# Two MLPs behind hashed attention on one core: products with v in threes, a narrower hash with bits through DRAM, 128-row rounding, copies per PSUM tile

## The chip, the cores and the metric

The kernel runs on one core of a Trainium2 chip. The metric is the device time of one execution in microseconds, as the median of repeated runs.

## What is computed

Attention for 2 batches of 8 heads (16 heads of 768 positions, width 64). Six random projections of q and of k give each position a 6-bit bucket; a score counts only where the buckets of the two positions agree. Then two MLPs over 1536 tokens (512 to 2048 to 512), the first with softplus, the second with hard swish.

```python
q_bits = (np.einsum('bhsd,dk->bhsk', q, proj) > 0)      # 6 bits; likewise k_bits
mask = q_bucket[:, :, :, None] == k_bucket[:, :, None, :]
scores = scale * np.matmul(q, k.transpose(0, 1, 3, 2))
scores = np.where(mask, scores, -1000000000.0)
attn = softmax(scores);  x = attn @ v                    # to (1536, 512)
h = x @ w1_in;  x = softplus(h) @ w1_out
h = x @ w2_in;  out = (h * np.clip(h + 3, 0, 6) / 6) @ w2_out
```

## The kernel before

A planner (`Schedule.run`) writes out the instruction order of every engine before anything runs: each operation has a cost per engine, a due time (`prio`, from `WHEN`, `TH`, `STEP`, ...) and dependencies, and the planner repeatedly gives the engine that would end first its most urgent operation that is ready. `SAME` and `CROSS` are what it charges from an operation's end to its follower on the same or on another engine, `STAY` what a change between kinds of matmul (scores, transposes, column tiles) adds to the due time. Each engine then runs its list strictly in order.

*Preparation of a head* (`prepare`, lines 302 to 415). Numbers are split into a rounded high part and a remainder, so that matmuls of the fast type keep precision. `raw` holds k in rows 0 to 63 and q in rows 64 to 127, `rawk` holds k twice. ACT writes q's high part scaled (line 337) and k's high part twice (`ka`, line 249). DVE writes q's remainder (line 344) and k's remainder (line 254, `kb`) in two 64-row operations. One DMA copies q's high part to `qb` (line 366). The hash (line 379) multiplies `raw` with a sign matrix into two 64-column tiles of 384 columns, side by side in PSUM; DVE turns the sums into bits (line 401, `bt`), and four DMAs spread the bits over rows 64 to 95 of `qb` and `kb` (line 410). Head 0 has no time for DMAs: its four quarters of bits are written by DVE (line 391), each from 32 rows.

*Attention of a head* (`attend`, lines 420 to 536), in six tiles of 128 queries. Two matmuls per half of the keys give the scores (lines 437 and 438; the second one has remainders and bits, and takes the mask into the sum). DVE takes the maximum (451) and makes scale and bias for the exponential (458), ACT the exponential (466), TensorE six transposes (477), ACT or, for every third tile, ACT or DVE the copy into `et` (line 249 or 251). Products with v (493) run in column tiles of 64, two side by side, in groups of two key chunks, eight records each. Then the result goes through a copy, a transpose back (515) and the division (530), and every second head into the features `xh`, `xl` (557 and on).

*PSUM* has three double banks (`two0` to `two2`), which scores and transposes take in turn, so that three tiles form a batch, and two single banks (`av`, `pre`) for the products with v, the hash and the other transposes.

*The MLPs* run over 2 layers, 3 groups of 512 tokens and 16 slices of the hidden width: 12 matmuls into `ph` (662), the activation on ACT and DVE, 12 accumulating matmuls into two double banks (755 in the first layer, 757 in the second). Weights arrive as 64-bit floats and are converted on ACT and DVE; half of the first layer's blocks are converted during attention, the rest behind it. At a group's end `finish` copies the four sums of 512 columns one by one.

## Time and profile before

| what | value |
|---|---|
| median of 3 runs | 785.51 us (785.46 to 785.63) |
| profiled execution: its own time | 787.35 us |
| its span, first instruction to last | 785.6 us |
| granted TensorE clock, mean | 0.998 |
| PE busy | 764.9 us, 97% |
| DVE busy | 529.0 us, 67% |
| ACT busy | 485.0 us, 62% |

The span is what the engines' instructions cover; the profiled execution takes 1.7 us more around it. Busy shares are means over stages that differ: attention up to some 245 us, the MLPs behind it. A matmul's end is modelled, so TensorE counts as busy through short waits; the start of the next instruction tells more than the length of one.

### The profile page before, as it was taken

How to read it: one execution, taken by the hardware profiler on the slowest of the kernel's cores; microseconds unless marked ns; L12 is line 12 of the kernel's file. 1: busy time of each engine (PE TensorE's matmuls, PEld its weight loads, DVE VectorE, ACT ScalarE, POOL GpSimd, SP SyncE). 2: the span in 40 equal slices, each digit the busy share in tenths (PEclk: the TensorE clock that was granted, in tenths of full speed). 3: DMA queues.
4: the chain of work that ended last, by engine and by line, in shares of the span. 5: the costliest groups of instructions: out<-in, count | busy, mean ns of one | idle time of the engine just before them, and what ended most of it. 6: DMA issues, size and time to landing. Idle time of an engine off the chain costs nothing.

```text
span 785.6 us, 10356 instructions
## 1 busy us (share of the span) xinstructions
PE 764.9 (97%) x3808; PEld 599.1 (76%) x3808; DVE 529.0 (67%) x938; ACT 485.0 (62%) x821; POOL 9.5 (1%) x53
## 2 busy tenths in 40 slices
PE   4999999999999999999999999999999999999997
PEld 2677677677668788878888788878888888888886
DVE  6698887888986999964545899999932222232222
ACT  3789999998988778665556678766622322232222
POOL 1000000000000000000000000000000000000000
PEclk9999999999999999999999999999999999999999
DMA  5354454353323070000000555530000100010001
GB/s 165 108 162 116 115 165 120 110 163 118 80 73 134 28 294 1 1 0 1 1 0 1 188 196 191 177 107 1 1 0 14 42 0 1 1 53 1 1 0 54
DMA packets 26354, 58.61 MB, mean 75 GB/s; under 512 B 3584, under 2 KB 7552, under 8 KB 26304
## 3 DMA queue, kind: packets, MB, share of 16 engines
q1 hardware_dynamic: 22128, 49.56, 19.7%
q10 hardware_dynamic: 4176, 8.39, 3.4%
q8 instruction: 30, 0.49, 0.3%
q14 instruction: 20, 0.16, 0.1%
HBM read 48.89 MB, written 3.15 MB: 66 GB/s over the span
## 4 chain that ended last, share of the span: by engine, by line
PE 90%; ACT 4%; DVE 3%; issue 2%; DMA 1%; SPq 0%; ACTq 0%; DVEq 0%
PE ph L662 34%; PE acc L755 17%; PE acc L757 17%; PE tp L477 7%; PE av L493 6%; PE sc L437 4%; PE sc L438 3%; ACT e L466 2%; DVE nm L451 2%; PE xt L557 1%; ACT ka L249 1%; PE pt L515 1%; PE d L379 1%; DMA raw<-in_q_dram 1%; ACT et L249 0%
## 5 line engine op out<-in xcount | busy, mean ns | idle before, releaser
L662 PE MATMUL ph<-xh,w 128*128 128x512 f32 x768 | 239.1, 393 | 0.0
L662 PEld LDWEIGHTS ph<-xh,w 128*128 128x128 f32 x768 | 143.8, 188 | 31.7
L662 PE MATMUL ph<-xl,w 128*128 128x512 f32 x384 | 150.2, 391 | 0.0
L691 DVE SCALAR_TENSOR_TENSOR ml<-me,ph 128x512 f32<-128x512 f32 x48 | 33.1, 690 | 116.0 <-ACT me L686 115.8
L686 ACT ACTIVATE me<-ph,three 128x512 f32<-128x512 f32 x48 | 33.0, 687 | 124.2 <-PE ph L662 120.7
L466 ACT ACTIVATE e<-sc,bs 128x768 f32<-128x768 f32 x96 | 94.0, 986 | 19.0 <-DVE bs L458 19.0
L451 DVE TENSOR_REDUCE nm<-sc 128x1 f32<-128x768 f32 x96 | 88.7, 951 | 20.8 <-PE sc L438 20.6
L755 PE MATMUL acc<-gh,w 128*128 128x512 f32 x384 | 98.8, 395 | 0.1
L757 PE MATMUL acc<-w,gh 128*128 128x512 f32 x384 | 97.4, 392 | 0.0
L477 PEld LDWEIGHTS tp<-ident,e 128*128 128x128 f32 x576 | 63.3, 142 | 29.3 <-ACT e L466 20.2
L755 PEld LDWEIGHTS acc<-gh,w 128*128 128x128 f32 x384 | 70.9, 188 | 19.1 <-ACT gh L249 2.8
L757 PEld LDWEIGHTS acc<-w,gh 128*128 128x128 f32 x384 | 72.1, 188 | 16.2
L662 PEld LDWEIGHTS ph<-xl,w 128*128 128x128 f32 x384 | 72.1, 188 | 16.0
L477 PE MATMUL tp<-ident,e 128*128 128x128 f32 x576 | 76.6, 281 | 4.9 <-ACT e L466 3.8
L437 PE MATMUL sc<-ka,qa 128*128 128x384 f32 x192 | 69.1, 360 | 0.1
L493 PE MATMUL av<-et,vx 128*64 128x384 f32 x384 | 68.8, 494 | 0.0
L438 PE MATMUL sc<-kb,qb 96*128 96x384 f32 x192 | 65.3, 340 | 0.8 <-DVE kb L391 0.7
L249 ACT ACTIVATE et<-tp 128x768 f32<-128x768 f32 x82 | 62.2, 815 | 2.4 <-PE tp L477 2.3
L722 DVE SCALAR_TENSOR_TENSOR me<-mu,me 128x512 f32<-128x512 f32 x48 | 33.3, 693 | 33.1 <-ACT mu L717 33.0
L249 ACT ACTIVATE gh<-ml 128x512 fp32r<-128x512 f32 x48 | 30.2, 629 | 38.8 <-DVE ml L734 38.6
L755 PE MATMUL acc<-gl,w 128*128 128x512 f32 x192 | 53.4, 392 | 0.7 <-ACT xh L249 0.7
L757 PE MATMUL acc<-w,gl 128*128 128x512 f32 x192 | 53.1, 391 | 0.0
(65 smaller groups left out, 957.8 us busy)
## 6 DMA issues: line engine op xcount, KB each, us to landing
raw<-in_moe_w_out_dram SPq DMA_DIRECT2D x30, 512.0 KB, 3.5
raw<-in_moe_w_in_dram SPq DMA_DIRECT2D x18, 512.0 KB, 4.3
raw<-in_moe_w_in_dram ACTq DMA_DIRECT2D x14, 512.0 KB, 4.8
rawk<-in_kv_dram SPq DMA_DIRECT2D x15, 384.0 KB, 5.0
raw<-in_kv_dram SPq DMA_DIRECT2D x16, 192.0 KB, 3.2
raw<-in_q_dram SPq DMA_DIRECT2D x16, 192.0 KB, 3.7
vx<-in_kv_dram SPq DMA_DIRECT2D x16, 192.0 KB, 3.0
out_dram<-y SPq DMA_DIRECT2D x12, 256.0 KB, 2.1
```

The source lines that it names most:

```text
L249: nc.scalar.activation(out, in_, AF.Copy)
L437: nc.tensor.matmul(o, qa[h].ap[:, qs], ka[h].ap[:, cs], start=True, stop=False)
L438: nc.tensor.matmul(o, qb[h].ap[0:KB, qs], kb[h].ap[0:KB, cs], start=False, stop=True)
L451: lambda e, sc=sc, t=t: nc.vector.reduce_max(nm.ap[:, t, 0:1], sc.ap[:, :, :HALF], axis=AX.XY, negate=True),
L466: lambda e, sc=sc, ex=ex, t=t: nc.scalar.activation(ex.ap.rearrange("p (u k) -> p u k", u=2), sc.ap[:, :, :HALF], AF.Exp, bias=bs.ap[:, t, ...
L477: nc.tensor.transpose(o, ex.ap[:, c * P : (c + 1) * P], ident.ap)
L493: nc.tensor.matmul(av.ap[u * D : (u + 1) * D, :HALF], vx[h].ap[:, c, :], et[u].ap[:, c, :], start=(c == 0), stop=(c == NT - 1),)
L662: nc.tensor.matmul(bank(), w[:, a, :], x[b].ap[:, kc, :], start=(kc + i == 0), stop=(kc == KC - 1 and i == 2))
L691: lambda e: nc.vector.scalar_tensor_tensor(l.ap, e1.ap, 6.0, bank(), op0=ALU.min, op1=ALU.mult),
L722: lambda e: nc.vector.scalar_tensor_tensor(e1.ap, u.ap, -1.0, e1.ap, op0=ALU.add, op1=ALU.subtract),
L755: nc.tensor.matmul(o, w.ap[:, a, cs], b.ap, start=st, stop=sp)
L757: nc.tensor.matmul(o, b.ap[:, cs], w.ap[:, a, :], start=st, stop=sp)
```

## The change

Seven things change. The planner's constants and due times are replaced; it may now prefer a more urgent operation that becomes ready a little later (`LOOK`), charges more for following a result on DVE itself (`SAME`), and holds back DVE from operations that ACT could do (`LEAN`). The hash of heads 1 to 15 runs in four tiles of 32 columns over 192 positions each. Its bits take 16 rows instead of 32 per kind, are written to DRAM in one DMA and read back in two. One ACT operation over 128 rows makes the high parts of k and scaled q, with a column `both` as the scale; one DVE operation makes both remainders into `kb`, from where a DMA moves q's remainder to `qa`. Products with v go in groups of three key chunks. The scores of head 0 wait only for the halves of bits that they read, and head 0's loads go to ACT's queue. In the MLPs, sums are copied per PSUM tile of two banks, the first products of a group are split by tile, and the last group's columns run in the order 2, 0, 1, 3. Any tile's copy into `et` may go to DVE.

```diff
+GROUP = 3
...
-SAME = dict(A=0.13, D=0.05, P=0.1, T=0.0, S=0.0, H=0.0)
+SAME = dict(A=0.13, D=0.12, P=0.1, T=0.0, S=0.0, H=0.0)
-STAY = 10.971
+STAY = 38.792
+LEAN = 8.449
+LOOK = dict(A=0.248, D=0.161, T=0.042)
...
-                        options.append((op.prio, at, at + end, unit, e, op))
+                        options.append((op.prio, at, at + end, unit, e, op, LEAN if e == "D" and len(op.cost) > 1 else 0.0))
...
-            end, unit = min((o[2], o[3]) for o in options)
+            end, unit = min((o[2] + o[6], o[3]) for o in options)
...
-            rivals = [o for o in rivals if o[1] <= soon]
+            rivals = [o for o in rivals if o[1] <= soon + LOOK.get(unit, 0.0)]
...
-    KB = D + ROWS
+    BR = ROWS // 2
+    KB = D + BR
+    QT = S // 4
...
+    line = buffer("heads", [1, 2, P], F32, "line", 1, "line")
+    spread = buffer("rows", [1, 2, P], F32, "spread", 1, "spread")
+    quarters = buffer("heads", [P, 2], F32, "quarters", 1, "quarters")
...
+    def set_line(e):
+
+        low, high = (line.ap[:, i, :].rearrange("o (u r) -> o u r", r=ROWS) for i in range(2))
+        nc.gpsimd.memset(line.ap[:, 0, :], 0.0)
+        for first in (NB, BR):
+            nc.gpsimd.memset(low[:, :, first : first + NB], -TINY)
+        nc.gpsimd.memset(high[:, :, :BR], 1.0)
+        nc.gpsimd.memset(high[:, :, BR:], -BIG)
+
+    plan.add(dict(P=2.25), set_rows, writes=[thr, top], prio=-3)
+    plan.add(dict(P=0.75), set_line, writes=[line], prio=4)
+    plan.add(
+        dict(S=0.6),
+        lambda e: engines[e].dma_start(out=spread.ap, in_=line.ap), reads=[line], writes=[spread], prio=-20, dma=(0.1, 2.1),
+    )
+    plan.add(
+        dict(S=0.6), lambda e: engines[e].dma_start(out=quarters.ap, in_=spread.ap[0].rearrange("i p -> p i")),
+        reads=[spread], writes=[quarters], prio=-20, dma=(0.1, 2.6),
+    )
+    both = buffer("heads", [P, 1], F32, "both", 1, "both")
+
+    def set_both(e):
+        nc.gpsimd.memset(both.ap[0:D, :], 1.0)
+        nc.gpsimd.memset(both.ap[D:P, :], SCALE)
+
+    plan.add(dict(P=0.2), set_both, writes=[both], prio=-2)
...
+    def set_hash4(e):
+        nc.gpsimd.memset(hash4.ap, 0.0)
+        for n in range(2):
+            nc.gpsimd.tensor_copy(hash4.ap[:, n * BR : n * BR + NR], hashes.ap[:, n * ROWS : n * ROWS + NR])
+
+    plan.add(dict(P=0.9), set_hash4, reads=[hashes], writes=[hash4], prio=4)
...
-        first = queue if h > 1 else dict(S=0.6)
+        first = queue if h > 1 else dict(S=0.6) if h else dict(A=0.06)
...
-        plan.add(wide, scaled, reads=[raw], writes=[qa[h]], prio=at + WHEN["high_q"])
-        plan.add(
-            narrow,
-            lambda e: nc.vector.scalar_tensor_tensor(
-                qa[h].ap[0:D, :], raw.ap[D:P, :], SCALE, f32(qa[h].ap[D:P, :]), op0=ALU.mult, op1=ALU.subtract
-            ),
-            reads=[raw, qa[h]], writes=[qa[h]], prio=at + WHEN["low_q"],
-        )
         if h:
+            plan.add(
+                dict(A=0.864), lambda e: nc.scalar.activation(qa[h].ap, raw.ap, AF.Copy, scale=both.ap[:, 0:1]),
+                reads=[raw, both], writes=[qa[h]], prio=at + WHEN["high_q"],
+            )
+            plan.add(
+                queue, lambda e: engines[e].dma_start(out=f32(qb[h].ap[0:D, :]), in_=f32(qa[h].ap[D:P, :])),
+                reads=[qa[h]], writes=[qb[h]], prio=at + WHEN["copy_q"], dma=(0.8, 2.7),
+            )
+            rest = plan.add(
+                dict(D=0.93),
+                lambda e: nc.vector.scalar_tensor_tensor(
+                    kb[h].ap, raw.ap, both.ap[:, 0:1], f32(qa[h].ap), op0=ALU.mult, op1=ALU.subtract
+                ),
+                reads=[raw, both, qa[h]], writes=[kb[h]], prio=at + WHEN["low_q"],
+            )
+            moved = [
+                plan.add(
+                    queue, lambda e: engines[e].dma_start(out=f32(qa[h].ap[0:D, :]), in_=f32(kb[h].ap[D:P, :])),
+                    writes=[qa[h]], uses=[kb[h]], prio=at + WHEN["low_k"], dma=(0.8, 2.7), after=[rest],
+                )
+            ]
...
-        plan.add(
-            dict(D=0.85), lambda e: minus(e, kb[h].ap[0:D, :], raw.ap[0:D, :], f32(ka[h].ap[0:D, :])),
-            reads=[raw, ka[h]], writes=[kb[h]], prio=at + WHEN["low_k"],
-        )
...
+        def dot4(e):
+            for u in range(4):
+                nc.tensor.matmul(
+                    dots.ap[u * ROWS : (u + 1) * ROWS, :QT], hash4.ap, raw.ap[:, u * QT : (u + 1) * QT],
+                    start=True, stop=True,
+                )
...
                 for n, x in enumerate((qb, kb)):
-                    rows = slice((2 * u + n) * ROWS, (2 * u + n + 1) * ROWS)
-                    plan.add(
+                    rows = slice((2 * u + n) * ROWS, (2 * u + n) * ROWS + BR)
+                    parts[n, u] = plan.add(
...
-        bits = buffer("heads", [P, HALF], F32R, "bt", 2, f"bt{h}")
-        plan.add(
-            dict(D=0.585),
+        plan.add(dict(T=0.36), dot4, mode="c", reads=[raw, hash4], writes=[dots], prio=at + WHEN["dots"])
+        bits = buffer("heads", [P, QT], F32R, "bt", 2, f"bt{h}")
+        plan.add(
+            dict(D=0.386),
             lambda e: nc.vector.tensor_scalar(
-                bits.ap, dots.ap[:, :HALF], thr.ap[:, 0:1], top.ap[:, 0:1], op0=ALU.is_gt, op1=ALU.mult
+                bits.ap, dots.ap[:, :QT], quarters.ap[:, 0:1], quarters.ap[:, 1:2], op0=ALU.is_gt, op1=ALU.mult
             ),
-            reads=[dots, thr, top], writes=[bits], prio=at + WHEN["bits"],
-        )
-        for u in range(2):
-            for n, x in enumerate((qb, kb)):
-                plan.add(
-                    queue,
-                    lambda e, u=u, n=n, x=x: engines[e].dma_start(
-                        out=f32(x[h].ap[D:KB, u * HALF : (u + 1) * HALF]),
-                        in_=f32(bits.ap[(2 * u + n) * ROWS : (2 * u + n + 1) * ROWS, :]),
-                    ),
-                    reads=[bits], writes=[x[h]], prio=at + WHEN["send"], dma=(0.2, 1.95),
-                )
+            reads=[dots, quarters], writes=[bits], prio=at + WHEN["bits"],
+        )
+        sent = buffer("rows", [4, 2, BR, QT], F32, "sent", 2, f"sent{h}")
+        plan.add(
+            queue,
+            lambda e: engines[e].dma_start(out=sent.ap.rearrange("u n r c -> (u n r) c"), in_=f32(bits.ap)),
+            reads=[bits], writes=[sent], prio=at + WHEN["send"], dma=(0.4, 2.1),
+        )
+        for n, x in enumerate((qb, kb)):
+            plan.add(
+                queue,
+                lambda e, n=n, x=x: engines[e].dma_start(
+                    out=f32(x[h].ap[D:KB, :]).rearrange("r (u c) -> r u c", u=4),
+                    in_=sent.ap[:, n].rearrange("u r c -> r u c"),
+                ),
+                reads=[sent], writes=[x[h]], after=moved if n else (), prio=at + WHEN["send"], dma=(0.3, 2.5),
+            )
...
-                    reads=[qa[h], qb[h], ka[h], kb[h]], writes=[sc], prio=step + WHEN["scores"],
+                    reads=[qa[h], ka[h]], writes=[sc], uses=[qb[h], kb[h]], prio=step + WHEN["scores"],
+                    after=[
+                        op for i, x in enumerate((qb[h], kb[h])) for op in x.writers
+                        if op not in parts.values() or op is parts[i, (t // n, u)[i]]
+                    ],
...
-                reads=[sc], writes=[nm], prio=step + WHEN["max"],
-            )
-            plan.add(
-                dict(D=0.07),
+                reads=[sc], writes=[nm], prio=step + WHEN["max"], after=nm.writers[:1],
+            )
+
+
...
-                reads=[nm], writes=[bs], prio=step + WHEN["max"],
+                writes=[bs], prio=step + WHEN["max"], after=[nm.writers[-1]], uses=[nm],
...
-                dict(A=0.692) if t % 3 else dict(A=0.692, D=0.867), even, reads=[tp], writes=[et[t // n]], prio=step + WHEN["even"],
+                dict(A=0.692, D=0.867), even, reads=[tp], writes=[et[t // n]], prio=step + WHEN["even"],
...
-        for c in range(0, NT, 2):
+        for c in range(0, NT, GROUP):
             last = [
                 plan.add(
-                    dict(T=1.29), mode="c", emit=lambda e, c=c: [some(c), some(c + 1)],
+                    dict(T=0.645 * GROUP), mode="c", emit=lambda e, c=c: [some(c + i) for i in range(GROUP)],
...
+    def store(g, c, e, after, prio):
+        b, cc = divmod(4 * g + c, NT)
+        y = buffer("m", [P, 512], F32, "ye"[c // 2], 2, f"y{g}_{c}")
+        tile_of = acc[1, g][c // 2]
+        copied = plan.add(
+            {e: dict(A=0.478, D=0.602)[e]}, lambda e: cast(e, y.ap, tile_of.ap[:, c % 2, :]),
+            uses=[tile_of], writes=[y], prio=prio, after=after,
+        )
+        dst = out[b * S : (b + 1) * S, :].rearrange("(p c) e -> p c e", c=NT)[:, cc, :]
+        plan.add(
+            dict(S=0.6), lambda e: nc.sync.dma_start(out=dst, in_=y.ap), reads=[y], prio=prio, dma=(1.0, 2.1)
+        )
+        return copied
...
+        order = [(i, range(4)) for i in range(3)]
+        if f == 0:
+            order[:1] = [(0, (0, 1)), (0, (2, 3))]
+        if f == NF - 1:
+            order = [(i, [c]) for c in ((2, 0, 1, 3) if (layer, g) == (1, NG - 1) else range(4)) for i in range(3)]
...
-                    reads=[w, gl if i == 2 else gh], writes=acc[layer, g], prio=prio, after=last,
+                    reads=[w, gl if i == 2 else gh], writes=[acc[layer, g][c // 2] for c in cs[::2]] if len(cs) > 1 else acc[layer, g],
+                    prio=prio, after=last,
...
+            if (layer, g, cs, i) == (1, NG - 1, [2], 2):
+                early = store(g, 2, "D", last, prio)
+            if (layer, g, cs, i) == (1, NG - 1, [1], 2):
+                last = [*last, early]
...
-        for c in range(4):
-            o = lambda c=c: acc[layer, g][c // 2].ap[:, c % 2, :]
+        for i in range(2):
+            tile_of, ends = acc[layer, g][i], [done[layer, g, c] for c in (2 * i, 2 * i + 1)]
             if layer == 0:
-                place = lambda x, c=c: x[1, g].ap[:, c, :]
+                place = lambda x, i=i: x[1, g].ap[:, 2 * i : 2 * i + 2, :]
                 hi = plan.add(
-                    dict(A=0.478), lambda e, o=o, place=place: cast(e, place(xh), o()),
-                    uses=[acc[layer, g][c // 2]], writes=[xh[1, g]], prio=prio, after=[done[layer, g, c]],
+                    dict(A=0.905), lambda e, t=tile_of, place=place: cast(e, place(xh), t.ap),
+                    uses=[tile_of], writes=[xh[1, g]], prio=prio, after=ends,
                 )
                 plan.add(
-                    dict(D=0.602), lambda e, o=o, place=place: minus(e, place(xl), o(), f32(place(xh))),
-                    uses=[acc[layer, g][c // 2]], writes=[xl[1, g]], prio=prio, after=[hi],
-                )
+                    dict(D=1.135), lambda e, t=tile_of, place=place: minus(e, place(xl), t.ap, f32(place(xh))),
+                    uses=[tile_of], writes=[xl[1, g]], prio=prio, after=[hi],
+                )
+            elif g < NG - 1:
+                for c in (2 * i, 2 * i + 1):
+                    store(g, c, "AD"[i], ends, prio)
+            elif i == 0:
+                for c in range(2):
+                    store(g, c, "D", ends, prio)
             else:
-                b, cc = divmod(4 * g + c, NT)
-                y = buffer("m", [P, 512], F32, "ye"[c // 2], 2, f"y{g}_{c}")
-                plan.add(
-                    dict(A=0.478) if c % 2 else dict(D=0.602), lambda e, o=o, y=y: cast(e, y.ap, o()),
-                    uses=[acc[layer, g][c // 2]], writes=[y], prio=prio, after=[done[layer, g, c]],
-                )
-                dst = out[b * S : (b + 1) * S, :].rearrange("(p c) e -> p c e", c=NT)[:, cc, :]
-                plan.add(
-                    dict(S=0.6), lambda e, dst=dst, y=y: nc.sync.dma_start(out=dst, in_=y.ap),
-                    reads=[y], prio=prio, dma=(1.0, 2.1),
-                )
+                store(g, 3, "A", ends, prio)
 
 
     def time_of(layer, g, f):
```

## Rows read from the trace of the kernel before

**Rows 1.** Table of stages: PE, PEld, DVE, ACT, POOL busy us (instructions); clock; DMA; GB/s.

```profile
26.00:240.00 214.00, 209.94 (x1375) 152.88 (x1376) 180.21 (x340) 193.28 (x337) 6.68 (x28) 1.00 0.41 120
240.00:340.00 100.00, 100.00 (x459) 78.63 (x458) 91.21 (x166) 74.41 (x132) 0.33 (x2) 1.00 0.24 90
```

**Rows 2.** Timeline of TensorE's matmuls, one batch (start, us taken, engine, line, what).

```profile
109.63 1.51 PE L493 MATMUL av<-et,vx 128*64 128x384 f32 x8
110.97 0.81 PE L379 MATMUL d<-raw,hash 128*64 128x384 f32 x4
111.72 2.55 PE L477 MATMUL tp<-ident,e 128*128 128x128 f32 x18
```

**Rows 3.** Timeline of all engines in that batch.

```profile
108.33 1.82 DVE L451 TENSOR_REDUCE nm<-sc 128x1 f32<-128x768 f32 x2 [2.16 <-PE sc L438]
...
109.63 0.20 PEld L493 LDWEIGHTS av<-et,vx 128*64 128x64 f32 x4 [0.25 <-issue]
...
110.07 0.28 DVE L458 SCALAR_TENSOR_TENSOR bs<-nm 128x2 f32<-128x2 f32 x2
...
110.32 0.99 ACT L466 ACTIVATE e<-sc,bs 128x768 f32<-128x768 f32 x1
```

**Rows 4.** Waits, 40 to 240 us: total us, times, longest.

```profile
PEld tp L477 <- ACT e L466: 16.4, 32, 1.0
...
ACT e L466 <- DVE bs L458: 12.6, 11, 2.0
...
PE d L379 <- PE av L493: 2.3, 4, 0.6
```

**Rows 5.** Instructions grouped by shape, 40 to 200 us: busy us, mean ns; idle before.

```profile
L466 ACT ACTIVATE e<-sc,bs 128x768 f32<-128x768 f32 x67 | 65.6, 986 | 8.0 <-DVE bs L458 7.9
...
L249 ACT ACTIVATE et<-tp 128x768 f32<-128x768 f32 x58 | 43.8, 815 | 1.0 <-PE tp L477 1.0
...
L344 DVE SCALAR_TENSOR_TENSOR qa<-raw,qa 64x768 fp32r<-64x768 f32 x11 | 10.5, 953 | 0.3
L254 DVE TENSOR_TENSOR kb<-raw,ka 64x768 fp32r<-64x768 f32 x11 | 10.4, 941 | 0.0
...
L249 ACT ACTIVATE ka<-rawk 128x768 fp32r<-128x768 f32 x11 | 9.3, 843 | 3.4 <-PE sc L437 3.3
L337 ACT ACTIVATE qa<-raw 64x768 fp32r<-64x768 f32 x11 | 9.3, 843 | 0.3
...
L401 DVE TENSOR_SCALAR bt<-d,thr,top 128x384 fp32r<-128x384 f32 x12 | 8.0, 664 | 0.0
```

**Rows 6.** Timeline of all engines, 118 to 130 us.

```profile
119.07 0.95 DVE L344 SCALAR_TENSOR_TENSOR qa<-raw,qa 64x768 fp32r<-64x768 f32 x1
...
125.98 0.41 DVE L254 TENSOR_TENSOR xl<-xt,xh 128x256 fp32r<-128x256 f32 x1
...
126.50 0.87 PE L379 MATMUL d<-raw,hash 128*64 128x384 f32 x4 [0.58 <-PE av L493]
...
129.23 0.42 PE L437 MATMUL sc<-ka,qa 128*128 128x384 f32 x1
```

**Rows 7.** DMA issues, 40 to 200 us: count, size, median us to landing.

```profile
qb<-qa SPq DMA_DIRECT2D x11, 192.0 KB, 2.9
...
kb<-bt SPq DMA_DIRECT2D x23, 48.0 KB, 2.3
```

**Rows 8.** Timeline of all engines, start of the first head.

```profile
12.23 0.45 PE L438 MATMUL sc<-kb,qb 96*128 96x384 f32 x1 [0.75 <-DVE kb L391]
...
13.80 1.81 DVE L451 TENSOR_REDUCE nm<-sc 128x1 f32<-128x768 f32 x2
...
17.12 0.96 PE L477 MATMUL tp<-ident,e 128*128 128x128 f32 x6 [2.24 <-ACT e L466]
```

**Rows 9.** Timeline of all engines, a seam between token groups.

```profile
522.12 0.50 PE L755 MATMUL acc<-gl,w 128*128 128x512 f32 x1 [0.69 <-ACT xh L249]
```

**Rows 10.** Timeline of all engines, the end.

```profile
782.09 0.60 ACT L249 ACTIVATE y<-acc 128x512 f32<-128x512 f32 x1 [0.83 <-DVE y L251]
```

71 lines of the change are left out of this document (39 added, 32 removed).

## Prediction

> **What bounds the kernel now.** I read the page's engine shares first, then the table of stages, then the matmul timeline of one attention head, then the waits. The reader is to see four things.
>
> First, TensorE is busy nearly throughout at full granted clock: 209.94 of 214 us in the attention stage, 100.00 of 100 behind it [rows 1]. So time is saved only where TensorE does less or waits less, and a wait may hide inside "busy", because matmul ends are modelled.
>
> Second, attention is tight on three engines at once. From 26 to 240 us ACT is busy 193.28 us and DVE 180.21, 90% and 84%. A full head has 94 matmul records (24 scores, 36 transposes, 24 products with v, 3 + 3 smaller transposes, 4 of the hash), so 1375 of them are 14.6 heads, and a head takes 214 / 14.6 = 14.6 us [rows 1].
>
> Third, TensorE works in batches of three query tiles: scores, then products with v (and the hash) as filler, then transposes that need the exponentials. The filler lasts from 109.63 to 111.72, of which the hash takes 110.97 to 111.72 [rows 2]. Meanwhile the first exponential starts only at 110.32, because DVE runs two maxima back to back (1.82 us from 108.33) before it makes the first scale and bias at 110.07 [rows 3].
>
> Fourth, the transposes wait for these exponentials: 32 weight loads in 200 us, 16.4 us in all. ACT itself stood idle 12.6 us there for DVE's scale and bias [rows 4]. Behind attention TensorE is busy 100.00 of 100 us [rows 1]: only seams between token groups and the end can give anything there.
>
> **The change part by part, for 15 heads (the first keeps its old form).**
>
> *Hash.* Two 64-column tiles of 384 columns become four 32-column tiles of 192. Now four records take 110.97 to 111.72 = 0.75 us. In the products with v ahead of them eight records, four side-by-side pairs, take 109.63 to 110.97 = 1.34, 0.335 a pair; so the hash is two pairs, 0.67, and 0.08 for leaving to the full-width transposes [rows 2]. With half the columns a pass takes 0.17 if four tiles run side by side as two do: 0.34 + 0.08 = 0.42, 0.33 saved. But the hash then has another tile width than the products beside it, one more change of form; I price it like the one that shows, 0.08. So 0.25 x 15 = 3.8 us. Bounds: no fewer columns in sum, so 0 if the tiles queue up; 0.33 x 15 = 5.0 if the extra change is free.
> The Trainium skill (TensorEngine Tiling (Array Packing), Key Properties) speaks against this part: changing the tiling mode, not merely the tile, drains TensorE. The 0.08 in the trace is the size of such a drain; without the rule the hash would give 5.0 and the sum would come to 12.5 us.
>
> *Products with v in threes.* The same 24 matmuls per head in two groups instead of three. In this stretch they already make two visits a head (one of 16 records, one of 8), so I credit no saved visit. What moves is filler: a batch with 8 records and the hash has 2.1 us of filler [rows 2], with 12 and the short hash 2.0 + 0.4 = 2.4; the other batch loses as much.
>
> *Waits for exponentials.* With the new planner constants (a lookahead for DVE and ACT, a higher cost of following one's own result) I expect a tile's scale and bias right behind its maximum. Then the first exponential starts about one maximum earlier, 1.82 / 2 - 0.1 = 0.8 us [rows 3]. What is to be won: a weight load of the filler stands idle 0.25 with nothing to wait for [rows 3]; the 32 waits average 16.4 / 32 = 0.51 [rows 4], so (0.51 - 0.25) x 32 = 8.3 us over 200 / 14.6 = 13.7 heads, 9.1 over 15. The cover of the shorter filler is thin, so I take 40%: 3.6. Bounds 0 and 9.1.
>
> *The hash's PSUM wait.* Every other head the hash starts late: at 126.50, 0.58 us idle, just after DVE's 0.41 us subtraction from 125.98 gave its bank back [rows 6]; the releaser shown there is an old matmul, so I read it as DVE. Four such waits cost 2.3 us [rows 4], 2.5 over 15 heads. DVE gets freer, but nothing orders it otherwise: a third, 0.8. Bounds 0 and 2.5.
>
> *One 128-row operation for the rounded parts.* ACT's 64-row and 128-row copies both take 843 ns, so rows are free; I carry this over to DVE. DVE loses the subtraction for k, 941 ns, and keeps the other, 953 [rows 5]. The bits over half the columns fall from 664 ns by an estimated 0.2 (between 0 and 0.33). That is 1.1 us per head of DVE, off TensorE's path: worth nothing directly, but DVE may now take any transpose eviction, which costs ACT 815 ns; that relieves ACT. ACT's copy now scales by a column of numbers; no row has that shape. The nearest pair is exponential 986 against eviction 815, so 0 to 0.17; I take 0.1, and it hides under ACT's 10% of idle [rows 1, 5]. If that is used up, 0.1 x 15 = 1.5 us come back.
>
> *Bits through DRAM and the moved part of q.* Per head the transfers stay five: out go four of 48 KB, in come one write, two reads and one 192 KB move. Landing takes 2.3 us for the bits' present transfer and 2.9 for a 192 KB copy [rows 7]. The chain becomes DVE subtraction, move, bits into kb. In the trace the subtraction runs 119.07 to 120.02 and its head's first scores at 129.23 [rows 6]: 9.2 us, needed 2.9 + 2.3 = 5.2. So 4.0 us of slack, cost 0. On SP the next head's two loads of raw data are queued behind the move and the wait for it; they are wanted a head later. The write and read back, at the same landing about 5 us instead of 2.3, run while the previous head's scores still hold the buffers.
>
> *Start.* The fourth score matmul waits 0.75 us for the second half of k's bits, third in DVE's order of four parts; the new dependencies let scores start on the halves they need, 0.7 earlier. The first transpose sits idle 2.24 us for an exponential after two maxima back to back from 13.80 [rows 8]; scale and bias between them give 0.8 to 0.9. Together 1.6; bounds 0 and 0.75 + 2.24 = 3.0.
>
> *Seams and end.* At 522.12 an accumulation waits 0.69 us for a copy out of its bank, and at the end the last ACT copy starts 0.83 us late, behind a DVE copy of the same PSUM tile [rows 9, 10]. Copies per tile, split first products and the new order of columns take both away: 1.5; bounds 0 and 1.5. The POOL set-up work and small loads added at the start hide behind the 12 us until head 0's scores run [rows 8].
>
> *Sum.* 3.8 + 3.6 + 0.8 + 1.6 + 1.5 = 11.3 us. The profiled span is 785.6 and the median of the runs shown 785.51, the same within 0.1; so 785.6 - 11.3 = 774.3 us. With every bound at nothing 785.6, with every bound full 5.0 + 9.1 + 2.5 + 3.0 + 1.5 = 21.1 less, 764.5.
>
> **The rivals.**
>
> *Saved and given back to the exponentials.* If ACT, at 90%, sets the batch time, TensorE's shorter hash only lengthens its wait at the transposes. For it: 32 waits for ACT already [rows 4]. Against it: DVE has 16% idle and loses 1.1 us per head, so it can take evictions. Only start, seams and about 1 us would stay: 785.6 - 1.6 - 1.5 - 1 = 781.5.
>
> *Four tiles in a queue.* If they don't run side by side, or the change of form costs the 0.33, the hash gives nothing: 774.3 + 3.8 = 778.1. For it: nothing here shows four tiles; against it: pairs do run so [rows 2].
>
> *Slower: k's bits come late.* The place is the first scores of a head. If DVE makes the 128-row subtraction one batch later, 14.6 / 2 = 7.3 us, the 4.0 us of slack turn into a wait of 3.3 us on TensorE. That eats the 11.3 us from 4 heads on; on five heads 774.3 + 16.5 = 791. For it: the subtraction is now two parts in one that both must wait for, and DVE serves it between blocks of maxima; against it: the slack, and DVE's idle share.
>
> DVE at 91.21 of 100 us behind attention [rows 1] may give back up to 3 us, if TensorE arrives there earlier than the converted weights: 777. It lies inside the likeliest case's own range.
>
> **How the numbers follow.** Likeliest, as summed, 767 to 780: 0.65. Given back, 780 to 784.5: 0.15. Tiles in a queue: 0.12. Late bits: 0.08. Of the second, a quarter falls within 0.2% (1.6 us, about what a measurement of this kernel can tell from no change), so faster 0.87, same 0.05, slower 0.08. The range 766 to 784 leaves out the slower case, the weakest gains and a gain near all upper bounds, some 0.17 together.
>
> **What would show it.** Right: hash records that end after about 0.42 us; scale and bias behind each single maximum; fewer and shorter waits of transposes for exponentials; a head in about 14 us; no accumulation wait at the group seams; the last copy straight behind the last matmul. Wrong: score matmuls that wait for a DMA into kb, hash records one after the other, ACT above 95% with the same waits, or TensorE idle for weights behind 240 us.

## The result, and the profile of the kernel after

The changed kernel takes 775.38 us (median of 4 runs, 774.21 to 776.89) against 785.53 (785.46 to 785.63): ratio 0.9872, 95% interval 0.9852 to 0.9891, so 1.3% faster, clear of the noise. The forecast was 774.3, in the range 766 to 784, so both the sign and the size are right. What has to be shown is whether the terms were. Several were not, and their errors offset one another.

The two profiled executions must be set side by side with care. Before took 787.35 us with a span of 785.6, after 774.67 with a span of 773.0; so each has 1.7 us around its span, and the spans differ by 12.6 us where the medians differ by 10.15. That is because the execution of before lies 1.8 us above its median and that of after 0.7 below. The forecast set the span of before against the median of the runs and found them the same: they agree by chance.

First the path of TensorE in the two traces, as four times from the matmul timeline (us):

```
                                      before    after   gained
first scores of head 1                 27.50    26.89     0.6
from there to first scores of head 15 202.94   192.48    10.5
from there to end of last matmul      550.83   549.12     1.7
from there to end of span                4.3      4.5    -0.2
```

Second, the stretch of fourteen whole heads, cut up: each matmul is given the time from its start to the start of the next one, and these are summed by what the matmul makes (us per head). In this reckoning a wait belongs to the work ahead of it.

```
                  scores  products  transposes   hash  smaller      sum
                            with v  of exp.             transposes
before              4.63      4.34        4.21   0.66        0.67   14.50
after               4.68      4.17        3.93   0.40        0.57   13.75
```

The four differences that matter are hash 0.26, transposes 0.28, products with v 0.17 and smaller transposes 0.10; scores give 0.05 back. Hash and products have to be read together: the time for leaving column tiles to the transposes stands in the hash's column in before, where the hash comes last, and in the products' in after. Where nothing waits, a head's products and hash take 1.34 + 0.75 [rows 2] + 2.73 = 4.82 us in before, the last number from this line up to the transposes at 119.39:

```profile
116.66 2.80 PE L493 MATMUL av<-et,vx 128*64 128x384 f32 x16
```

In after they take 0.46 + 2.09 + 2.09 = 4.64 (timeline below; the second batch has the same 2.09, 125.68 to 127.77). So the hash itself saves 0.18 us, and the rest of the two columns is waiting that is gone.

Now the views that answer to those of before. The table of stages of after, as [rows 1]:

```profile
26.00:240.00 214.00, 213.90 (x1479) 159.86 (x1479) 200.52 (x366) 191.38 (x334) 6.48 (x30) 1.00 0.50 141
240.00:340.00 100.00, 99.77 (x441) 77.98 (x441) 91.75 (x156) 72.83 (x124) 0.00 (x0) 1.00 0.17 64
```

TensorE was 4.06 us short of the stage's 214 and is 0.10 short now. DVE rose from 180.21 to 200.52 us (94%), though each head spares it 1.1 us: more of the heads' work fits into the stage, and it takes evictions that were ACT's.

The matmul timeline of after in a batch with the hash, as [rows 2]:

```profile
117.53 0.33 PE L513 MATMUL sc<-kb,qb 80*128 80x384 f32 x1
117.80 0.53 PE L448 MATMUL d<-raw,hash 128*32 128x192 f32 x8
118.26 2.16 PE L574 MATMUL av<-et,vx 128*64 128x384 f32 x12
120.35 1.53 PE L558 MATMUL tp<-ident,e 128*128 128x128 f32 x12
```

Eight hash records take 117.80 to 118.26, 0.46 us; the forecast was 0.42. The hash now stands between scores and products instead of behind the products. Twelve products follow as filler, 2.09 us.

All engines in a batch of after, as [rows 3]:

```profile
110.18 0.94 DVE L530 TENSOR_REDUCE nm<-sc 128x1 f32<-128x768 f32 x1
...
111.15 0.16 DVE L539 SCALAR_TENSOR_TENSOR bs<-nm 128x2 f32<-128x2 f32 x1
...
111.22 0.95 DVE L530 TENSOR_REDUCE nm<-sc 128x1 f32<-128x768 f32 x1
...
111.50 1.00 ACT L547 ACTIVATE e<-sc,bs 128x768 f32<-128x768 f32 x1
```

One maximum, then scale and bias at 111.15, then the next maximum: the exponential starts 0.38 us after its own maximum ends, where two maxima came first in [rows 3].

Waits of after from 40 to 240 us, as [rows 4]:

```profile
PEld tp L558 <- issue: 13.2, 22, 0.6
...
ACT e L547 <- DVE bs L539: 4.5, 8, 1.7
...
PEld d L448 <- issue: 2.7, 11, 0.3
...
PEld tp L558 <- ACT e L547: 1.8, 3, 0.6
```

The transposes' waits for exponentials went from 16.4 us (32 times) to 1.8 (3 times), ACT's for scale and bias from 12.6 to 4.5. The hash waits only for its own issue; the 2.3 us behind products are gone. The first line is new (3.6 us, 6 times, in before): the weight load of the transposes stands idle 0.6 us on the average even where it waits for nothing. So idle time of a weight load is not time that TensorE loses. What it loses shows in the matmuls: eighteen transposes with nothing to wait for take 1.93 to 1.94 us in both traces (127.30 to 129.23 in before, 113.55 to 115.49 in after), and 2.30 in [rows 2]'s batch.

Instructions of after by shape, 40 to 200 us, as [rows 5]:

```profile
L255 ACT ACTIVATE et<-tp 128x768 f32<-128x768 f32 x48 | 38.5, 810 | 7.2 <-PE tp L558 7.2
...
L257 DVE COPY et<-tp 128x768 f32<-128x768 f32 x24 | 23.0, 957 | 2.2 <-PE tp L558 1.0
...
L399 DVE SCALAR_TENSOR_TENSOR kb<-raw,both,qa 128x768 fp32r<-128x768 f32 x11 | 11.2, 1019 | 0.6
...
L390 ACT ACTIVATE qa<-raw,both 128x768 fp32r<-128x768 f32 x11 | 10.3, 936 | 3.5 <-PE sc L512 3.5
...
L471 DVE TENSOR_SCALAR bt<-d,quarters 128x192 fp32r<-128x192 f32 x11 | 5.2, 469 | 0.0
```

The 128-row remainder costs DVE 1019 ns against 953 for 64 rows and a constant, ACT's scaling by a column of numbers 936 against 843, and the bits 469 against 664: forecast were no rise, a rise by 0.1 and a fall by 0.2. DVE evicts 24 transposes here, and ACT 48 instead of 58.

DMA issues of after, 40 to 200 us (count, size, median us to landing), as [rows 7]:

```profile
qa<-kb SPq DMA_DIRECT2D x11, 192.0 KB, 2.9
sent<-bt SPq DMA_DIRECT2D x11, 96.0 KB, 2.4
...
kb<-sent SPq DMA_DIRECT2D x12, 48.0 KB, 3.3
```

The matmuls of the first head in after, as [rows 8]:

```profile
11.17 0.69 PE L512 MATMUL sc<-ka,qa 128*128 128x384 f32 x1
12.87 0.66 PE L513 MATMUL sc<-kb,qb 80*128 80x384 f32 x1 [1.01 <-DVE kb L460]
13.32 0.53 PE L512 MATMUL sc<-ka,qa 128*128 128x384 f32 x1
...
15.90 0.53 PE L512 MATMUL sc<-ka,qa 128*128 128x384 f32 x1
...
16.99 0.87 PE L558 MATMUL tp<-ident,e 128*128 128x128 f32 x6 [0.31 <-ACT e L547]
```

The wait for k's bits did not go: it moved from the fourth score matmul (0.75 us) to the second (1.01 us), and the scores run every 0.32 us, where later on one follows the other after 0.18. This is taken up below.

And the end of after, all engines, as [rows 10]:

```profile
767.18 2.85 SPq L834 DMA_DIRECT2D out_dram<-y  x4
...
767.85 1.29 DVE L257 COPY y<-acc 128x512 f32<-128x512 f32 x2 [0.69 <-PE acc L852]
...
768.10 0.39 PE L852 MATMUL acc<-w,gl 128*128 128x512 f32 x1
768.57 0.60 ACT L255 ACTIVATE y<-acc 128x512 f32<-128x512 f32 x1 [3.43 <-DVE y L257]
```

The last copy starts 0.47 us after the last matmul starts, where it started 1.21 after it (780.88 to 782.09, [rows 10] for the copy). The span still ends 4.5 us after the last matmul.

### The profile page after: what moved, and what is told of

The parts are those of the page before. It is cut to its first block, busy times and chain, and to the rows that moved or that the text cites. A ratio compares the mean times of both kernels' runs of the same rounds, so it can differ in the third digit from the quotient of the medians.

```text
span 773.0 us, 10533 instructions
## 1 busy us (share of the span) xinstructions
PE 756.3 (98%) x3868; PEld 597.3 (77%) x3868; DVE 544.7 (70%) x939; ACT 477.1 (62%) x793; POOL 10.3 (1%) x63
## 4 chain that ended last, share of the span: by engine, by line
PE 88%; DVE 8%; ACT 2%; issue 1%; DMA 1%; DVEq 0%; ACTq 0%
PE ph L743 30%; PE acc L852 17%; PE acc L850 13%; PE av L574 9%; PE tp L558 9%; PE sc L512 4%; PE sc L513 4%; DVE me L811 1%; DVE bits L707 1%; DVE me L803 1%; DVE ml L815 1%; DVE bits L714 1%; PE xt L638 1%; PE d L448 1%; DVE gl L260 1%
## 5 line engine op out<-in xcount | busy, mean ns | idle before, releaser
L530 DVE TENSOR_REDUCE nm<-sc 128x1 f32<-128x768 f32 x96 | 91.2, 950 | 4.0 <-PE sc L513 3.9
L558 PE MATMUL tp<-ident,e 128*128 128x128 f32 x576 | 73.8, 276 | 2.1 <-ACT e L547 1.9
L513 PE MATMUL sc<-kb,qb 80*128 80x384 f32 x192 | 66.4, 346 | 1.0 <-DVE kb L460 1.0
L255 ACT ACTIVATE et<-tp 128x768 f32<-128x768 f32 x61 | 49.0, 809 | 8.9 <-PE tp L558 8.9
```

What stands on the lines that cost most here:

```text
L255: nc.scalar.activation(out, in_, AF.Copy)
L513: nc.tensor.matmul(o, qb[h].ap[0:KB, qs], kb[h].ap[0:KB, cs], start=False, stop=True)
L530: lambda e, sc=sc, t=t: nc.vector.reduce_max(nm.ap[:, t, 0:1], sc.ap[:, :, :HALF], axis=AX.XY, negate=True),
L558: nc.tensor.transpose(o, ex.ap[:, c * P : (c + 1) * P], ident.ap)
```

## The experiments

Unless it is said otherwise, an experiment keeps the order in which all engines of the kernel that it starts from work, and alters only what is issued in one place; and it is compared by the table per head, whose rows for all of them are these (with the median of the time, and its ratio to before with the interval):

```
                  scores  prod.  transp.  hash  smaller    sum   median  ratio
after, again        4.68   4.17     3.93  0.40     0.57  13.75   776.52  0.9872 [0.9859, 0.9886]
max_in_pairs        4.69   4.22     4.37  0.40     0.56  14.23   784.25  0.9974 [0.9963, 0.9984]
dve_extra           5.06   4.17     4.24  0.40     0.57  14.44   786.12  0.9998 [0.9989, 1.0006]
evict_third         4.85   4.17     3.97  0.40     0.58  13.96   778.45  0.9898 [0.9884, 0.9911]
hash_wide           4.68   4.13     3.92  0.60     0.57  13.90   778.47  0.9900 [0.9886, 0.9913]
hash_twice          4.68   4.17     3.92  0.68     0.57  14.01   778.71  0.9910 [0.9897, 0.9924]
uneven              4.69   4.20     4.46  0.40     0.57  14.31   783.54  0.9966 [0.9953, 0.9978]
before_single_max   4.59   4.39     4.31  0.66     0.63  14.58   786.95  1.0010 [1.0001, 1.0019]
pairs               4.77   4.52     4.55  0.40     0.62  14.86   791.20  1.0068 [1.0055, 1.0082]
warm                4.86   4.22     4.34  0.41     1.15  14.98   796.49  1.0127 [1.0112, 1.0143]
warm_kept           4.68   4.17     3.93  0.40     0.57  13.75   775.53  0.9862 [0.9848, 0.9875]
```

**The changed kernel again.** 

> The changed kernel once more. If its executions spread by over 2 us again, as the four shown (774.2 to 776.9) do against 0.2 us of the kernel before, the spread belongs to the kernel and not to a chip; I expect a median of 774.5 to 776.5 and a profiled execution in which head 15's first scores stand within 1 us of 219.4.

The fourteen heads take 192.51 us, as in the first execution (192.48): order-keeping edits can be told apart to some hundredths per head. All that differed was the start (below): head 15's first scores come at 221.06, 1.7 us later than in the first execution, and the median, 776.52, lies just above the expected range. The four times (775.55 to 776.79) spread by 1.2 us, and 18 times of before on the same chip by 1.6 (785.76 to 787.38); so the spread is not the changed kernel's alone.

**Scale and bias held back behind a second maximum.** For tiles 0 and 3 the scale and bias wait until the next maximum is out, or until their exponential needs them; 28 of the 32 pairs of maxima of before come back.

```diff
-  scale_bias(t)
+  held.append(scale_bias(t)) if t % 3 == 0 else scale_bias(t)   # issued behind the next maximum
```

> The changed kernel with the planner's order kept, except that the first scale and bias of most batches goes behind the second maximum again. If earlier exponentials carry much of the gain (the 3.6 us of the sum), it is 3 to 5 us slower than the changed kernel and transposes wait for exponentials over 8 us between 40 and 240 us again. The rival, that DVE's and ACT's lighter load carries it, expects under 1 us and under 4 us of such waits.

The heads take 199.27 us, 6.8 more, and all of it but 0.05 a head stands at the transposes (3.93 to 4.37). Its waits, 40 to 220 us:

```profile
PEld tp L564 <- ACT e L553: 11.3, 24, 1.1
ACT e L553 <- DVE bs L545: 9.3, 14, 1.8
```

In the same stretch after has 1.8 (3 times) and 2.1 (6 times). The mechanism is the one forecast, but the price is more than the 3 to 5 us expected: the transposes lose 0.44 a head by this edit, where they won only 0.28 against before.

**The same edit on the kernel before.** Its scale and bias for tile t go ahead of the maximum of tile t + 1, with everything else in its order.

```diff
-  maximum(t);  ...  scale_bias(t - 1)
+  scale_bias(t - 1);  maximum(t)
```

> The kernel before with its order kept, except that each scale and bias follows its own maximum. If earlier exponentials alone carry the gain, 4 us or more faster than the kernel before, and far fewer waits of transposes for exponentials. If they pay only together with DVE's lighter load and the even filler, under 2 us faster, or slower, since DVE stands waiting for its own maximum.

It gains nothing: fourteen heads take 204.03 us, 1.1 more than before, and the transposes still wait for exponentials, 40 to 220 us:

```profile
PEld tp L484 <- ACT e L473: 16.5, 29, 0.6
...
ACT e L473 <- DVE bs L445: 6.3, 17, 1.5
```

Before has 13.3 us (26 times) and 10.1 (9 times) there. ACT waits less and TensorE does not. So an early scale and bias is needed in the changed kernel, and not enough in the old one: taken alone, in the old order, it is not worth the 3.6 us at which it was put. What a new order of the old operations would make of it was not tried.

**DVE's spared operation given back.** The 128-row remainder of k and q is computed twice, with the same result; the extra 1.02 us a head is about what the change took from DVE by the rows shown, 941 + 195 - 66 = 1070 ns.

```diff
-  nc.vector.scalar_tensor_tensor(kb[h].ap, raw.ap, both.ap[:, 0:1], ...)
+  [nc.vector.scalar_tensor_tensor(kb[h].ap, raw.ap, both.ap[:, 0:1], ...) for _ in range(2)]
```

> The changed kernel with the 128-row remainder computed twice (1.02 us more of DVE per head, order of all engines kept). If DVE's lighter load carries the gain, most of it goes: 7 to 10 us slower than the changed kernel. If DVE only has to stay below saturation, the price is what its idle 0.9 us per head (187.94 us busy of 200) does not take, plus lateness within batches: 1 to 4 us.

It costs nearly the whole gain of the heads, as the first of the two expectations had it: 202.16 us, 9.7 more, and no difference from before in the time. The scores lose 0.38 a head, the transposes 0.31. New waits, 40 to 220 us:

```profile
PEld sc L512 <- DVE et L257: 4.5, 7, 1.2
...
PE sc L512 <- DVE et L257: 2.7, 7, 0.9
```

The scores wait for the eviction that gives them their banks. In after DVE is busy 170.93 of the 180 us, which leaves 0.7 us a head, less than the operation takes. So in this order nearly all of the gain hangs on the saving that was counted as "worth nothing directly".

**Evictions of two tiles in three back to ACT,** as before.

```diff
   def even(e, tp=tp, t=t):
+      e = "A" if t % 3 else e
```

> The changed kernel with order kept, but evictions of two tiles in three forced onto ACT, as before the change. If the freedom to evict on DVE carries the gain, 4 us or more slower than the changed kernel. If the earlier exponentials carry it, under 2 us: ACT has 21 us of idle in 200.

3.0 us over the heads, between the two expectations, and most of it at the scores (0.17 a head). DVE falls from 170.93 to 156.35 of 180 us, ACT rises from 162.64 to 168.87, and now DVE waits for scores, 40 to 220 us:

```profile
DVE nm L530 <- PE sc L513: 12.4, 15, 1.2
```

(2.5 us, 8 times, in after.) So the relief of ACT is worth about 0.2 us a head in this order.

**The hash in two 64-column tiles again,** with bits of 384 columns, through DRAM as after.

```diff
-  plan.add(dict(T=0.36), dot4, ...);  bits = [P, QT]
+  plan.add(dict(T=0.36), dot, ...);   bits = [P, HALF]
```

> The changed kernel with order kept and bits still through DRAM, but the hash in two 64-column tiles of 384 columns and the bits made over 384 columns, as before. If the shorter hash shortens TensorE's path, 3 to 5 us slower than the changed kernel at 0.3 us a head. If it is given back at the transposes, under 1 us. DVE's 0.2 us more per head is part of it: by the measured price of 9.6 us for 1.02 us a head it alone would be worth 1.9 us, so that 5 to 6 us would be both.

2.15 us over the heads: the hash's own time rises by 0.20 a head, of which the products give 0.04 back. DVE pays 0.2 a head more for the wider bits here, and TensorE's other times hold still, so the price is that of the columns. It is less than the 3 to 5 us expected, and the 1.9 us expected for DVE's part did not come: 0.2 us fits into the 0.7 a head that DVE has left. The stretch holds twelve hashes: each takes 0.70 us instead of 0.46, and the twelve products behind it 2.04 instead of 2.09, a net 0.19.

**The four small tiles twice.** The second round writes the same sums.

```diff
-  for u in range(4):
+  for u in (*range(4), *range(4)):
```

> The changed kernel with the narrow hash computed twice into the same bank (order kept, the first result is overwritten). On TensorE alone it adds 8 records, two passes of 0.16 us if four tiles run side by side: 15 x 0.32 = 4.8 us if TensorE sets the pace, under 1 us if DVE does, which is busy 95% there. If the tiles queued up, 15 x 1 = 15 us.

The matmul timeline has the sixteen records in one stretch:

```profile
119.63 0.86 PE L448 MATMUL d<-raw,hash 128*32 128x192 f32 x16
120.42 2.16 PE L574 MATMUL av<-et,vx 128*64 128x384 f32 x12
```

Sixteen take 0.79 us and eight 0.46, so a round of eight costs 0.33. Two rounds of four side by side, at half of the 0.335 of a 384-column pair [rows 2], make 0.335; eight in pairs would make 0.67. Four tiles run side by side. The fourteen heads take 196.19 us, 3.7 more than in after; the twelve extra rounds in them would be 4.0 at 0.33 each. So TensorE sets the pace here.

**Filler split unevenly.** The 24 products of a head are issued as 8 and 16 records instead of 12 and 12.

```diff
-  [some(c + i) for i in range(GROUP)]
+  [some(i) for i in ((0, 1), (2, 3, 4, 5))[c // GROUP]]
```

> The changed kernel with order kept, but of a head's six key chunks the first group of products runs two and the second four, so that the fillers of the two batches are as uneven as before the change (8 and 16 records). If the even filler carries part of the gain, heads 1 to 15 take 3 us or more longer than 192.5 us. If the pairs planned anew were slow for their new order alone (208.0 us there), this one stays within 1 us.

7.9 us over the heads, again at the transposes (4.46). Its matmul timeline, where a batch has eight products as filler:

```profile
115.71 1.51 PE L574 MATMUL av<-et,vx 128*64 128x384 f32 x8
117.15 1.59 PE L558 MATMUL tp<-ident,e 128*128 128x128 f32 x12
```

Its waits, 40 to 220 us:

```profile
PEld tp L558 <- ACT e L547: 19.3, 37, 0.8
```

The batch with eight records comes to its transposes 0.65 us earlier (1.44 us of products for 2.09), before its exponentials are there. Twelve each suit both batches, in an order that was planned for twelve: the 7.9 us may be more than what the threes bring.

**Pairs, planned anew.** The planner gets groups of two and makes another order.

```diff
-GROUP = 3
+GROUP = 2
```

> The changed kernel with products with v in groups of two key chunks again, planned anew with the same constants. I credited the threes nothing: under 1 us, either way. If the even filler of both batches carries part of the gain, 3 us or more slower, with waits of transposes for exponentials over 6 us between 40 and 220 us.

208.03 us for the heads, worse than before, with transposes, products and scores all longer; in this plan TensorE comes to the products 42 times in the fourteen heads instead of 28. It shows nothing of pairs alone, for the next one, also planned anew, with an edit that should touch the start only, does as badly.

**TensorE warmed at the start, planned anew,** by six unused matmuls of zeros into a bank that the scores use later.

```diff
+  for _ in range(6):
+      plan.add(dict(T=0.64), matmul of zeros into "two2", prio=-9999)
```

> The changed kernel with six extra matmuls on zeros ahead of the first hash, their result unused, planned anew. The two profiled executions of the changed kernel differ by 1.66 us at head 1's first scores (26.89 and 28.55) and by nothing after. If that is TensorE's clock, still at its lower level while head 0's scores run, these matmuls raise it earlier: 1 to 2 us faster, and executions within 0.5 us of one another. If the spread comes from the loads, no gain and the same spread.

209.71 us for the heads, 17 more than after; smaller transposes alone cost 1.15 a head. It seems that the constants suit one list of operations. What a new plan costs hides any effect of some tenths, and this run tells nothing of the clock.

**The same warming, in the order of after.** Unused matmuls of zeros: eight ahead of the first hash, two behind the hash of head 1.

```diff
   def dot(e):
+      warm(8, slice(0, HALF))
   ...
+  if h == 1:
+      warm(2, slice(QT, 512))
```

> The changed kernel with order kept and ten matmuls on zeros put among TensorE's first ones (eight before the first hash, two behind the second; results unused). Head 1's first scores, at 26.9 to 28.6 us so far, come at 25.5 to 26.5, and heads 1 to 15 stay at 192.5: 1.5 to 2.5 us faster than the changed kernel, and executions within 0.6 us of one another. If the slowness of the same idea planned anew (209.7 us for heads 1 to 15) came from the matmuls themselves, it is over 10 us slower.

The heads keep their 192.51 us. Its matmuls in the first head:

```profile
12.46 0.41 PE L523 MATMUL sc<-kb,qb 80*128 80x384 f32 x1 [1.21 <-DVE kb L470]
...
14.43 0.34 PE L522 MATMUL sc<-ka,qa 128*128 128x384 f32 x1
...
16.54 0.88 PE L568 MATMUL tp<-ident,e 128*128 128x128 f32 x6 [1.59 <-ACT e L557]
```

The scores have the full pace, but the first transposes still start at 16.54, after 1.59 us of waiting for an exponential (16.99 and 0.31 in after). Head 1 starts at 26.44 instead of 26.89. Its times, 774.46 to 776.25, lie among those of after: the expected 1.5 to 2.5 us did not come, and the executions lie 1.8 us apart, not 0.6.

**And the last store issued by ACT's queue** instead of SP's, on top of the warming.

```diff
-  nc.sync.dma_start(out=dst, in_=y.ap)
+  (nc.scalar if (g, c) == (NG - 1, 3) else nc.sync).dma_start(out=dst, in_=y.ap)
```

> The same, and the last of the output transfers is issued by ACT instead of waiting its turn on SP. If the end is held up by SP's issues, 0.4 to 0.7 us faster than the one without; if by the transfers' own bytes and landing, under 0.2 us.

774.65 us (774.55 to 775.93), ratio 0.9856 [0.9842, 0.9869]: not to be told from warm_kept. From the end of the last matmul to the end of the span it has 4.40 us against 4.47. In this execution the warming did not even hold: the scores have the full pace, but by the trace's records of the clock the level falls at 16.47 us, at the end of a wait of 1.58 us for an exponential, and comes back at 19.88. The table of stages has it too (granted clock in the third column from the right):

```profile
10.00:20.00 10.00, 7.83 (x46) 5.45 (x44) 7.79 (x14) 3.90 (x7) 0.00 (x0) 0.83 0.76 203
```

## Why the prediction was right, and where its terms were off

**The hash: right in kind, somewhat too large.** Forecast 0.25 us a head. The column of the hash fell by 0.26, but 0.18 is what remains when hash and products are taken together (4.82 to 4.64 above), and hash_wide has 0.19 a hash where only the columns are undone: over 15 heads 2.8 us instead of 3.8. Two changes of form stand around it: the last scores are 0.27 us ahead of it (117.53 to 117.80) where one follows the other after 0.17; and behind it, 0.46 us for eight records are 0.13 more than the round of 0.33. The first of them stood ahead of the products in before too (109.37 to 109.63). The Trainium skill (TensorEngine Tiling (Array Packing), Key Properties) says that changing the tiling mode drains TensorE; the trace agrees in that each change costs about 0.1 us, and the sum had counted 0.08. That four tiles would queue is refuted by hash_twice.

**Waits for exponentials: the size by luck, wrong in what they hang on.** Forecast 3.6 us over 15 heads; the transposes fell by 0.28 a head, 4.2 over 15. The 3.6 were 40% of a bound of 9.1, and that bound was double what there was to win: it took 0.25 us, read at a weight load of the products, as the idle time without a wait, where the transposes have 0.6. At 1.94 us for eighteen, the 28 stretches of fourteen heads would take 54.3 us; before has 58.9 and after 55.0, so 4.6 were lost and 3.9 of them are won. The picture was that scale and bias behind each maximum would bring it. The runs show four conditions that must hold together in this order: taking back any one of early scale and bias, even filler, DVE's spared operation or free evictions loses 6.8, 7.9, 9.7 and 3.0 of the 10.5 us. These sum to 27, so no share can be put on one of them; and on the kernel before, early scale and bias alone gains nothing. What the new order gives without these four was not tried. The step that failed here is the pricing part by part: the products in threes and DVE's 1.1 us were put at nothing, because the one saves no visit (it doesn't: TensorE comes to the products 28 times in fourteen heads in both traces) and the other is off TensorE's path. But the threes make the filler of the two batches 2.55 us with the hash (117.80 to 120.35) and 2.09 without, where it was 2.09 and 2.73. In after DVE is busy 95% of the 180 us, and it is not off the path.

**The hash's wait for its bank: too small.** Forecast 0.8, bound 2.5. In before the eight products ahead of a hash take 1.34 us, but 2.08 to 2.10 four times in the fourteen heads; in after no such stretch is left. That is 3.0 us, 3.2 over 15: all of [rows 6]'s wait went. The forecast reason, a freer DVE, was not tried by itself; the hash now also stands in another place.

**Smaller transposes and scores: not forecast.** 0.10 a head won, 0.05 lost, 0.7 us in sum over the fourteen heads. The three that turn a result back stand between other transposes now (0.33 us, 108.25 to 108.58) instead of between scores and products (0.42, 102.24 to 102.66 in before); the rest was not looked into.

**Start: wrong.** Forecast 1.6 us of gain; the profiles show 0.6, and with before's execution 1.8 us above its median that is no gain at all: heads, MLPs and end make 10.5 + 1.7 - 0.2 = 12.0, the medians differ by 10.15, so as an estimate the start costs 1.9 us at the medians. The step that failed is "scores start on the halves they need, 0.7 earlier". Two things now stand ahead of the bits. The first hash starts later:

```profile
8.89 1.55 PE L441 MATMUL d<-raw,hash 128*64 128x384 f32 x4 [8.89 <-DVE hash L332]
```

In before the same view has it at 7.44:

```profile
7.44 2.83 PE L379 MATMUL d<-raw,hash 128*64 128x384 f32 x8 [7.44 <-DVE hash L295]
```

DVE's first work on q, which waits for its load, starts at 6.57 us instead of 6.09, and DVE now makes q's remainder (7.17, 0.95 us) before the sign matrix that the hash needs (8.13). Then DVE in the first head of after goes on so:

```profile
10.33 1.00 DVE L399 SCALAR_TENSOR_TENSOR kb<-raw,both,qa 128x768 fp32r<-128x768 f32 x1
11.37 0.67 DVE L460 TENSOR_SCALAR qb<-d,thr,top 16x384 fp32r<-16x384 f32 x1
12.05 1.39 DVE L460 TENSOR_SCALAR kb<-d,thr,top 16x384 fp32r<-16x384 f32 x2
```

Head 1's 128-row remainder, 1.00 us, runs ahead of head 0's bits. In before the bits of q and k start at 9.38 and 10.08, 2.0 us earlier. The other half of the term did come: from the first bits to the first transposes it is 5.6 us (11.37 to 16.99) instead of 7.7, which only makes up for the later bits.

TensorE's clock comes on top. In after the scores follow each other after 0.32 us until 16.22 and after 0.18 from 20.26 on. In the second execution of after the low pace lasts longer:

```profile
16.91 2.82 PE L558 MATMUL tp<-ident,e 128*128 128x128 f32 x12 [0.24 <-ACT e L547]
19.66 0.87 PE L448 MATMUL d<-raw,hash 128*32 128x192 f32 x8
...
21.64 0.42 PE L512 MATMUL sc<-ka,qa 128*128 128x384 f32 x1
```

Twelve transposes take 2.75 us where 1.5 is usual, and head 1 starts at 28.55 instead of 26.89: 1.66 us, which is the difference of the two spans (1.6). The profiled execution of before has its low pace elsewhere: its scores run at 0.18 us, and then TensorE, which has just waited 2.24 us for an exponential [rows 8], is at the lower level during the transposes. Its table of stages, with the granted clock, 0.50, third from the right:

```profile
17.80:21.10 3.30, 3.30 (x16) 3.10 (x15) 1.31 (x2) 2.17 (x6) 0.00 (x0) 0.50 0.91 225
```

The first eighteen transposes take 3.36 us there (17.12 to 20.48) instead of 1.94, 1.4 of the 1.8 us by which this execution lies above its median. In before_single_max, which is before but for the place of scale and bias, and where the level did not fall, head 1 starts at 26.12 instead of 27.50; in warm_kept, which is after with full pace, at 26.44. So with full pace on both sides the start gains nothing, as far as one execution each can tell: DVE's chain of bits, maxima and exponentials still sets the first transpose.

**Seams and end: half of the sum.** Forecast 0.7 and 0.8; found 1.7 for all behind head 15's first scores, of which that head itself should be 0.75 (counted with the heads) and leaves about 0.95 for the seams, and -0.2 for the end. No accumulating matmul waits for a copy out of its bank any more; 0.2 us once for another operation of ACT is all that is left. The last copy does start earlier, as forecast: it ends 1.07 us after the last matmul's start instead of 1.81. But the last two copies now end together, at 769.14 and 769.17, where before had them at 782.00 and 782.69. Their stores of 256 KB are issued at 769.20 and 769.62, and by the trace's records of the landings they land at 771.28 and 771.96. In warm_tail two queues issue them at 769.80 and 769.85, and they land at 772.00 and 772.59. So the second one lands 0.6 to 0.7 us behind the first, whichever queue issues it: the transfers hold up the end, not the issues. From the last copy's end to the last landing it is 2.79 us instead of 2.06, which is what the earlier copy had gained.

**The rivals.** Saved and given back: no, the waits for exponentials fell to 3. Tiles in a queue: no. k's bits late: no score matmul waits for a DMA in 40 to 240 us. SP itself does wait for the move (waits of SP's queue in after, 40 to 240 us), at no cost to the heads:

```profile
SPq L485 <- DMA qa<-kb: 18.6, 13, 3.0
```

The forecast total thus came out well by luck: terms too large (the start by about 3.5 us at the medians, seams and end by 0.75) met terms too small: the heads, put at 3.8 + 3.6 + 0.8 = 8.2 us for fifteen, give 15 x 0.75 = 11.2.

## What to carry to other kernels

Where TensorE, DVE and ACT are all above 84% busy in one loop, price the batch and not the parts: write down what each engine must finish before the transposes, and ask of each spared operation what it lets come earlier, even if it is "off the path". Early scale and bias, taken back in the new kernel, cost 6.8 us, and put into the old one gained nothing; so both edits are needed before a part is given a price. Read what an engine loses from the starts of its matmuls, not from the idle time of its weight loads. And to undo one part of a scheduled kernel, keep the order of all engines and alter only what is issued: a new plan of nearly the same list cost 15 to 17 us here, more than the whole change.

## What the runs showed of the hardware that was not expected

Four 32-column tiles of 192 columns do run side by side: eight records in 0.33 us, with about 0.1 us for each change of form around them. DVE's remainder with a column of numbers as the scale and twice the rows costs 0.07 us more (1019 against 953 ns) where no rise was forecast; ACT's scaling by such a column costs 0.09 (936 against 843), about as forecast. Of two stores of 256 KB the second lands 0.6 to 0.7 us behind the first, from one queue or from two.

The clock at the start moves executions of one kernel apart. By the pace of the matmuls the first head of after runs at the lower of the two levels (1.2 and 2.4 GHz) until 16.2 us in one execution and about 21.6 in another; TensorE had been busy 1.1 to 1.2 us in the first ten in both. The table of stages gives 1.00 for 10 to 20 us in both, and that is no contradiction: the trace's records of the granted clock begin only at 16.48 and 21.63 us, with the upper level, and what lies ahead of the first record reads 1.00 in the table. There the pace of equal matmuls (0.32 or 0.18 us) has to be read. The experiments that keep the order of after fit: where the records begin at 15.9 to 16.5 us, head 1 starts at 26.8 to 27.3 (after, hash_twice, max_in_pairs), and where they begin at 20.3 to 21.6, at 27.7 to 28.8 (after_again, uneven, evict_third, hash_wide, dve_extra). The kernel before has its own spread: later runs of it reach from 785.5 to 787.4 us. What raises or lowers the level at a given time was not settled: it fell at the end of a wait of 1.58 us in warm_tail and 0.6 us after one of 2.24 in before, and a wait of 1.59 in warm_kept left it as it was.
